# Block attention and a gated feed-forward in one kernel: score order in the opening, and weight casts on GpSimd

## The chip, the cores and the metric

The kernel runs on one core of one Trainium2 chip. The metric is the device time of one execution in microseconds (us). The engines are TensorE (PE; PEld is its weight load), VectorE (DVE), ScalarE (ACT), GpSimd (POOL) and SyncE (SP), which issues the DMAs. Each engine works off its own queue in order; engines wait for each other through semaphores.

## The reference

```python
# attention: q, k, v are [8, 8, 576, 64], float32; block = 64
scores = scale * np.matmul(q, k.transpose(0, 1, 3, 2))
scores = np.where(block_i >= block_j, scores, -1000000000.0)
attn = np.exp(scores - np.max(scores, axis=-1, keepdims=True))
attn = attn / (np.sum(attn, axis=-1, keepdims=True) + 1e-09)
x = np.matmul(attn, v)                      # heads side by side: [8, 576, 512]
# feed-forward
h = gelu_tanh(x @ w_in)                     # [8, 576, 1024]
u, v = h[..., :512], h[..., 512:]
v_n = (v - mean(v)) / np.sqrt(var(v) + 1e-06) * g_ln
v_s = np.einsum('ts,bsd->btd', w_sg, v_n) + b_sg[None, :, None]
out = x + (u * v_s) @ w_out
```

`w_in` and `w_out` arrive as float64, everything else as float32.

## The kernel before, in words

**Numbers.** TensorE multiplies in a rounded 32-bit format, so each operand is split into a high part (a cast) and a low part (the rest, a subtraction), and three products are summed. Such splits are `qh`, `ql`, `kh`, `kl` (`split_qk`, line 111), `xh`, `xl` (`Values.split`, line 469) and the weights' `wi_h`, `wi_l`, `ws_h`, `ws_l`, `wo_h`, `wo_l` (`split_weight`, line 183). A piece of 128x256 doubles is first turned into singles by `from_f64` (line 187): one ScalarE step (the absolute value, scaled) and three VectorE integer steps, the last of which needs ScalarE's. Then the cast on ScalarE and the subtraction on GpSimd.

**Slots.** The work goes through 32 slots, one for a pair of heads of one batch; four slots are a batch. Slot n holds:

- the transposes `pA`, `pB`, `pC` of slot n's probabilities, with their copies to SBUF (`Values.turn`);
- the inverse sums `r` on VectorE and their spread `rx` on GpSimd (`inverse`, line 408), transposed into `pd` and `pe` (`turn_sums`);
- the scores of slot n+1 in two halves, called here the first scores (row blocks 4, 1 and 0) and the second scores (blocks 3 and 2). Each half is followed by masked maxima on VectorE (`maximum`) and exponentials with sums on ScalarE (`exponent`). Both are in `Scores`, as `first` and `second`;
- the values' products `ob` and `pe`, and the normalised result `x` on VectorE (`products`, `normalise`);
- the split of q and k for slot n+2 on GpSimd (`split_qk`), and in the next slot the split of `x`.

From slot 4 on, the feed-forward of the batch before is laid between these on TensorE by `hole`: five groups `accv`, eight `accu`, eight `accs`, eight `acco`. Between `accv` and `accs` stands a layer norm: moments and `centre` on VectorE, the inverse deviation `rs` on GpSimd, `scale` to `vh` and `vl` on ScalarE and VectorE. The first four slots have no feed-forward to lay in; there the kernel puts eight idle transposes of the identity ahead of `pd` (`warm` in `turn_sums`).

**What sets the order.** Up to slot 3 the queues of TensorE, VectorE, ScalarE and GpSimd follow the program text (`written`, line 50). From slot 4 on only TensorE does; the others, and the DMA queue always, are ordered by the framework's scheduler. `issue_after` puts weight steps behind named instructions.

**Weights.** `load_share` (line 681) takes steps of a list of weight pieces at places of a slot that the table `WS` sets: two of the eight `v` pieces of `w_in` in each of slots 0 to 3, then the eight `u` pieces, the spatial weights, and `w_out`. `need` takes a step more when a feed-forward part starts: the first `u` piece comes that way, at the start of slot 4.

**Banks.** PSUM has eight banks in one ring (`bank`): a new tile waits until the readers of the tile eight places earlier are done. `pB` of a slot takes the bank of the slot before's `pe`, which `x` reads last.

Of the kernel before, what the change touches and what calls it, by code (L numbers as in the profile page):

```python
# [20 lines left out]
def kernel(  # L21
# [14 lines left out]
    P = 128  # L36
# [74 lines left out]
    def split_qk(n):  # L111
        out = []
        for x, t in zip(raw.pop(n), "qk"):
            hi = sp.tile([P, S], F32R, tag=t + "h", name=t + "h", bufs=1)
            lo = sp.tile([P, S], F32R, tag=t + "l", name=t + "l", bufs=1)
            if n == 0:
                copy("v" if t == "q" else "a", hi, x)
                vector.tensor_tensor(lo, x, hi.bitcast(F32), op=ALU.subtract)
            else:
                copy("g", hi, x)  # L120
                gpsimd.tensor_tensor(lo, x, hi.bitcast(F32), op=ALU.subtract)
# [65 lines left out]
    def from_f64(raw, dh, dl, name):  # L187

        n = raw.shape[-1]
        words = raw.bitcast(U32).rearrange("p (n t) -> p n t", t=2)  # L190
        hi, lo = words[:, :, 1], words[:, :, 0]
        tm = page(U32, 2 * n, name)
        t, m = tm[:, :n], tm[:, n:]


        scalar.activation(m.bitcast(F32), hi.bitcast(F32), AF.Abs, scale=2.0**-112)

        vector.tensor_scalar(t, lo, 29, None, op0=ALU.logical_shift_right)
        vector.scalar_tensor_tensor(
            t, hi, 0x80000000, t, op0=ALU.bitwise_and, op1=ALU.bitwise_or  # L200
        )
        vector.scalar_tensor_tensor(
            t, m, 3, t, op0=ALU.logical_shift_left, op1=ALU.bitwise_or
        )
        split_weight(t.bitcast(F32), dh, dl)

    def load_weight(src, cols, dh, dl, name="w", ahead=2):

        W = 256
        parts = [(c, slice(f, f + W)) for f in range(cols.start, cols.stop, W) for c in range(NC)]  # L210
        raws = {}

        def fetch(k):
            if k < len(parts):
                c, fs = parts[k]
                raws[k] = page(src.dtype, W, name)
                nc.sync.dma_start(raws[k], src[c * P : (c + 1) * P, fs])

        for k in range(ahead):
            fetch(k)  # L220
        for k, (c, fs) in enumerate(parts):
            fetch(k + ahead)
            args = (raws.pop(k), dh[:, c, fs], dl[:, c, fs])
            if src.dtype == F32:
                split_weight(*args)
            else:
                from_f64(*args, name)
            yield True

    def load_spatial():  # L230
# [20 lines left out]
        for j in range(NT - 1):  # L251
# [15 lines left out]

    weights = deque(
        [
            ("v", load_weight(w_in, slice(DH, DFF), wi_h, wi_l)),  # L270
            ("u", load_weight(w_in, slice(0, DH), wi_h, wi_l)),
            ("s", load_spatial()),
            ("o", load_weight(w_out, slice(0, DM), wo_h, wo_l, "xr", 0)),
        ]
    )

    def weight_step():

        while weights and next(weights[0][1], None) is None:
            weights.popleft()  # L280

    def need(part):

# [3 lines left out]

    spill = {}
    xs = {}
    behind = {}  # L290

    class Scores:

# [71 lines left out]
        def first(self, between=None):
            parts = ((4, 0, SH), (1, 0, EXT[1])), ((4, SH, S), (0, 0, EXT[0]))
            if between is None:
                for p in parts:
                    self.step(*p)
            else:  # L370
                for p in parts:
                    self.products(*p)
                between()
                for p in parts:
                    self.softmax(*p)
# [12 lines left out]
    class Values:  # L388
# [27 lines left out]
                r.unsqueeze(2).broadcast_to([P, NT * 2, D]),  # L416
            )

        def turn_sums(self, idle):

            def spread(i):
                return self.rx[:, i, :]

            t, t2 = bank("pd"), bank("pe")
            warm(t2, idle)
            for a in (0, 1):
                turn(t[:, a * BLK : a * BLK + P], prob[a][0])
            for i in (0, 1, 2):
# [249 lines left out]
    WS = [(0, 2, 0, 0), (0, 2, 0, 0), (0, 2, 0, 0), (0, 2, 0, 0), (0, 4, 0, 2), (0, 2, 0, 1)]
    WS += [(0, 2, 1, 0), (0, 0, 0, 3), (0, 2, 0, 3), (0, 0, 0, 0)]

    def load_share(n, k):

        if n < len(WS):
            with ExitStack() as order:
                if n >= H // 2:
                    for ins in behind.values():
                        order.enter_context(tc.issue_after(ins.ins))
# [6 lines left out]
    def slot(n, sc):  # L694
        va = Values(n, sc)
        nx = n + 1 < N
        q = H // 2
        k = 6 if n // q == 1 else 3
        if n == q:
            written.intersection_update("P")  # L700
        g = [int(x) for x in (FIRST if n // q == 1 else PLAN)[n % q]]
# [22 lines left out]
        if n < q:
            nx = Scores(n + 1)
            nx.first(lambda: va.turn_sums(8))
        else:
            va.turn_sums(0)
            hole(g[2])
            run_gelu()  # L730
        load_share(n, 1)
        if nx and n >= q:
# [85 lines left out]
```

## Time and profile before

| | |
|---|---|
| median of 3 runs | 782.54 us (781.96 to 782.93) |
| profiled execution | 783.17 us, of which the span from first to last instruction is 781.4 us |
| mean granted TensorE clock | 0.989 of full |
| busy share of the span | PE 97%, PEld 92%, DVE 62%, ACT 55%, POOL 40% |
| HBM | 83 GB/s over the span |

The busy shares are averages over stages with different limits. A row of the timeline reads: start, time busy, engine, line, operation, out<-in, shapes, count, and in brackets how long the engine stood idle before it and what released it. All engine instructions go through one helper and so show line 60; they are told apart by their tiles.

### The profile page before, as it was taken

Reading aid. Unit: us, or ns where it says so; the run is one execution under the profiler, and the core shown is the slowest. Engines: PE = TensorE matmul, PEld = TensorE weight load, DVE = VectorE, ACT = ScalarE, POOL = GpSimd, SP = SyncE. Lnnn points to the kernel's source line nnn. Section 1 sums busy time; section 2 is a strip of 40 time slices with the busy share of each in tenths; the row PEclk is TensorE's granted clock in tenths of the full one; section 3 lists DMA queues with packets and bytes.
Section 4 is the critical chain, followed back from the end, with each engine's and each line's share of the span. In section 5 each row is a group of like instructions: output and inputs, shape, how many; then the busy total and the mean of one; then the engine's idle time right before and its main releaser. Section 6 shows DMA issues by size and latency. Waiting matters only on the chain.

```text
span 781.4 us, 18302 instructions
## 1 busy us (share of the span) xinstructions
PE 758.7 (97%) x7138; PEld 716.0 (92%) x7138; DVE 483.4 (62%) x1477; ACT 428.0 (55%) x1093; POOL 313.8 (40%) x385
## 2 busy tenths in 40 slices
PE   8878898999999999999999999999999999999998
PEld 8777797999999899998999999998999989998998
DVE  6667678866966439563694447763496634942632
ACT  5666595848753477336682377533774358720600
POOL 3453666754435224453233534332344513322121
PEclk9989999999999999999999999999999999999999
DMA  6325232323241113421232222321225112120042
GB/s 219 118 91 168 64 98 70 91 72 117 81 151 62 59 42 98 138 62 36 73 108 93 61 62 62 130 85 33 61 79 166 49 45 61 61 78 16 1 122 91
DMA packets 46922, 65.84 MB, mean 84 GB/s; under 512 B 4082, under 2 KB 22514, under 8 KB 46836
## 3 DMA queue, kind: packets, MB, share of 16 engines
q1 hardware_dynamic: 46836, 64.67, 26.5%
q8 instruction: 56, 0.92, 0.5%
q14 instruction: 30, 0.25, 0.1%
HBM read 45.78 MB, written 18.87 MB: 83 GB/s over the span
## 4 chain that ended last, share of the span: by engine, by line
PE 86%; DVE 5%; ACT 4%; POOL 2%; DMA 2%; issue 1%; SPq 0%; ACTq 0%; POOLq 0%; DVEq 0%
PE accs L60 15%; PE acco L60 13%; PE accv L60 12%; PE accu L60 12%; PE s L60 10%; PE ob L60 9%; PE pB L60 4%; PE pC L60 4%; PE pA L60 3%; ACT prob L60 3%; PE pd L60 2%; DVE prob L60 2%; PE pe L60 2%; DMA w<-in_w_in 1%; DVE vv L550 1%
## 5 line engine op out<-in xcount | busy, mean ns | idle before, releaser
L60 ACT ACTIVATE prob<-prob,negm 128x576 f32<-128x576 f32 (+3 forms) x320 | 176.3, 553 | 57.9 <-DVE negm L60 55.1
L60 DVE CUSTOM_DVE_ANT_0 prob<-s,mask 128x288 f32<-128x288 f32 (+3 forms) x320 | 121.5, 424 | 51.7 <-PE s L60 51.2
L60 POOL TENSOR_TENSOR xh<-x,xh 128x64 fp32r<-128x64 f32 x32 | 13.9, 435 | 184.9 <-DVE xh L60 115.2
L60 POOL TENSOR_TENSOR gl<-u,gh 128x288 fp32r<-128x288 f32 x64 | 52.4, 823 | 87.0 <-DVE gh L60 86.7
L60 PE MATMUL accu<-xh,wi_h 128*128 128x288 f32 x256 | 78.8, 308 | 0.0
L60 PE MATMUL accs<-ws_h,vh 128*128 128x288 f32 x256 | 77.8, 304 | 0.0
L60 PE MATMUL acco<-gh,wo_h 128*128 128x288 f32 x256 | 77.6, 303 | 0.0
L60 PE MATMUL accu<-xl,wi_h 128*128 128x288 f32 x256 | 76.0, 297 | 0.0
L60 PE MATMUL accu<-xh,wi_l 128*128 128x288 f32 x256 | 75.7, 296 | 0.0
L60 PE MATMUL accs<-ws_h,vl 128*128 128x288 f32 x256 | 75.5, 295 | 0.0
L60 PE MATMUL acco<-gl,wo_h 128*128 128x288 f32 x256 | 75.5, 295 | 0.0
L60 PE MATMUL accs<-ws_l,vh 128*128 128x288 f32 x256 | 75.5, 295 | 0.0
L60 PE MATMUL acco<-gh,wo_l 128*128 128x288 f32 x256 | 75.3, 294 | 0.0
L60 PE MATMUL accv<-wi_h,xh 128*128 128x512 f32 x160 | 66.0, 412 | 1.7 <-DVE x L60 1.5
L60 DVE TENSOR_TENSOR u<-accs,u 128x288 f32<-128x288 f32 x64 | 29.2, 457 | 56.3 <-PE accs L60 55.0
L60 PE MATMUL accv<-wi_l,xh 128*128 128x512 f32 x160 | 63.6, 398 | 0.0
L60 PE MATMUL s<-kh,qh 64*128 64x288 f32 (+4 forms) x384 | 63.0, 322 | 0.2 <-DVE negm L60 0.2
L60 ACT ACTIVATION_READ_ACCUMULATOR prob<-prob,negm 128x1 f32 x320 | 60.0, 188 | 0.0
L60 PE MATMUL s<-kh,ql 64*128 64x288 f32 (+4 forms) x384 | 58.7, 301 | 0.0
L60 PE MATMUL s<-kl,qh 64*128 64x288 f32 (+4 forms) x384 | 57.7, 300 | 0.1
L60 POOL CAST kh<-k_f 128x576 fp32r<-128x576 f32 x31 | 22.0, 710 | 84.4 <-PE s L60 73.1
L60 ACT COPY vv<-accv 128x512 f32<-128x512 f32 x32 | 18.6, 580 | 64.9 <-PE accv L60 64.9
(115 smaller groups left out, 2139.2 us busy)
## 6 DMA issues: line engine op xcount, KB each, us to landing
q_f<-in_qT SPq DMA_DIRECT2D x32, 288.0 KB, 2.9
k_f<-in_kT SPq DMA_DIRECT2D x32, 288.0 KB, 2.8
spill<-x SPq DMA_DIRECT2D x32, 288.0 KB, 3.2
xr<-spill SPq DMA_DIRECT2D x32, 288.0 KB, 2.9
out_T<-xr SPq DMA_DIRECT2D x32, 288.0 KB, 2.1
v_f<-in_v SPq DMA_DIRECT2D x32, 256.0 KB, 3.5
w<-in_w_in SPq DMA_DIRECT2D x16, 256.0 KB, 4.3
xr<-in_w_out SPq DMA_DIRECT2D x8, 256.0 KB, 2.6
```

What stands on the lines that cost most here:

```text
L60: return lambda *a, **k: pin(method(*a, **k), self.letter)
L550: tc.keep_in_program_order(nc.vector.scalar_tensor_tensor(x, x, stats[:rows, st, 0:1], g_bc[:rows, :], op0=ALU.subtract, op1=ALU.mult))
```

## The change

Four things change.

1. In slots 0 to 2 the second scores and their softmax stand ahead of the values' products and of `x`. In slot 3 `x` and its split still come ahead of the second scores. The eight idle transposes go. `opening_slot` is a function of its own now.
2. A weight piece is opened (loads, and the ScalarE step of a double) in one step and finished (three VectorE steps, cast, subtraction) in a second one. In slots 0 to 3 the opening stands behind `turn_sums` and ahead of the exponentials, and the finishing behind the first maxima. The eight `v` pieces are taken 3, 2, 2 and 1 a slot, not 2 a slot, and one more is loaded ahead.
3. The cast of a weight's high part goes from ScalarE to GpSimd, for all weights.
4. The inverse sums of slot n+1 are written ahead of the split of q and k at the end of slot n, from the end of slot 3 on; weight steps from slot 4 on are put behind the last GpSimd step of such a split, too. The table `WS` moves two pieces from slot 6 to slot 5.

```diff
     def split_weight(x, dh, dl):
-        scalar.copy(dh, x)
+        gpsimd.tensor_copy(dh, x)
         gpsimd.tensor_tensor(dl, x, dh.bitcast(F32), op=ALU.subtract)
...
+            opened = []
+            for j in range(k, k + size):
+                fetch(j + ahead)
+                raw = raws.pop(j)
+                opened.append(raw if src.dtype == F32 else Double(raw, name))
+            yield False
+            for j, x in zip(range(k, k + size), opened):
+                c, fs = parts[j]
+                split_weight(
+                    x if src.dtype == F32 else x.single(), dh[:, c, fs], dl[:, c, fs]
+                )
+            k += size
             yield True
...
-            ("v", load_weight(w_in, slice(DH, DFF), wi_h, wi_l)),
+            ("v", load_weight(w_in, slice(DH, DFF), wi_h, wi_l, "w", 3, (3, 2, 2, 1))),
...
-    WS = [(0, 2, 0, 0), (0, 2, 0, 0), (0, 2, 0, 0), (0, 2, 0, 0), (0, 4, 0, 2), (0, 2, 0, 1)]
-    WS += [(0, 2, 1, 0), (0, 0, 0, 3), (0, 2, 0, 3), (0, 0, 0, 0)]
+    WS = {
+        4: (0, 4, 0, 2),
+        5: (0, 5, 0, 0),
+        6: (0, 1, 0, 0),
+        7: (0, 0, 0, 3),
+        8: (0, 2, 0, 3),
+    }
...
+    def opening_slot(n, va):
+
+        va.turn(0, "A")
+        va.turn(1, "A")
+        split_pending()
+        va.turn(0, "B")
+        va.turn(1, "B")
+        va.inverse()
+        va.turn(0, "C")
+        va.turn(1, "C")
+        load_v(n + 1)
+        load_qk(n + 2)
+        nx = Scores(n + 1)
+        for p in nx.FIRST:
+            nx.products(*p)
+        va.turn_sums()
+        weight_half()
+        for p in nx.FIRST:
+            nx.softmax(*p)
+        weight_half()
+        if n < Q - 1:
+            nx.second()
+            va.products()
+            va.normalise()
+            pending.append(va.split)
+        else:
+            va.products()
+            va.normalise()
+            va.split()
+            nx.second()
+        nv = Values(n + 1, nx)
+        if n == Q - 1:
+            nv.inverse()
+        split_qk(n + 2)
+        return nx, nv
...
-        if n >= q:
-            va.inverse()
...
+        nv = None
+        if nx:
+            nv = Values(n + 1, nx)
+            nv.inverse()
         if n + 2 < N:
             split_qk(n + 2)
```

`Double` holds what `from_f64` did, in two parts: making one issues ScalarE's step, its `single` the three steps on VectorE. `weight_half` takes one of the two steps of a group of pieces.

On VectorE, the end of slot 1's weight steps and what follows. Before (`w` are the integer steps of a weight piece, `x` the result, the `ISA` rows the second maxima):

```order
L60 SCALAR_TENSOR_TENSOR w<-w 128x256 x2
L60 TENSOR_TENSOR x<-ob,rb 128x512
L60 TENSOR_TENSOR x<-pe,rb 128x64
L60 ISA prob_3_111,negm<-s,mask 128x448
L60 ISA negm 128x1
L60 ISA prob_3_121,negm<-s,mask 128x448
```

Now, in the same place:

```order
L60 SCALAR_TENSOR_TENSOR w<-w 128x256 x2
L60 ISA prob_3_111,negm<-s,mask 128x448
L60 ISA negm 128x1
L60 ISA prob_3_121,negm<-s,mask 128x448
L60 ISA negm 128x1
L60 ISA prob_2_109,negm<-s,mask 128x320
L60 ISA negm 128x1
L60 ISA prob_2_119,negm<-s,mask 128x320
L60 ISA negm 128x1
L60 TENSOR_TENSOR x<-ob,rb 128x512
```

The maxima of the second scores moved ahead of `x`, and no longer wait for the products that `x` reads.

On GpSimd, the same slot: `rx` are slot 1's inverse sums, `wi_l` the low parts of weights, `qh` to `kl` the split that slot 2's first scores read. Before:

```order
L60 COPY rx<-r 128x640
L60 MEMSET sums 128x2
L60 TENSOR_TENSOR wi_l<-w,wi_h 128x256 x2
L60 CAST qh<-q_f 128x576
L60 TENSOR_TENSOR ql<-q_f,qh 128x576
L60 CAST kh<-k_f 128x576
L60 TENSOR_TENSOR kl<-k_f,kh 128x576
```

Now:

```order
L60 COPY rx<-r 128x640
L60 MEMSET sums 128x2
L60 CAST wi_h<-w 128x256
L60 TENSOR_TENSOR wi_l<-w,wi_h 128x256
L60 CAST wi_h<-w 128x256
L60 TENSOR_TENSOR wi_l<-w,wi_h 128x256
L60 CAST qh<-q_f 128x576
L60 TENSOR_TENSOR ql<-q_f,qh 128x576
```

Two casts came in ahead of the split; the rest of the queue kept its order.

On GpSimd in slot 4: `xh`, `xl` split the last `x` of batch 0, `rx` are slot 4's inverse sums, `qh` to `kl` the split for slot 5, the `wi_l` rows weight pieces. Before:

```order
L60 TENSOR_TENSOR xl<-x,xh 128x576
L60 CAST qh<-q_f 128x576
L60 MEMSET sums 128x2
L60 TENSOR_TENSOR wi_l<-w,wi_h 128x256
L60 TENSOR_TENSOR ql<-q_f,qh 128x576
L60 CAST kh<-k_f 128x576
L60 COPY rx<-r 128x640
L60 TENSOR_TENSOR wi_l<-w,wi_h 128x256 x4
L60 TENSOR_TENSOR kl<-k_f,kh 128x576
```

Now:

```order
L60 TENSOR_TENSOR xl<-x,xh 128x576
L60 MEMSET sums 128x2
L60 COPY rx<-r 128x640
L60 CAST qh<-q_f 128x576
L60 TENSOR_TENSOR ql<-q_f,qh 128x576
L60 CAST kh<-k_f 128x576
L60 TENSOR_TENSOR kl<-k_f,kh 128x576
L60 CAST wi_h<-w 128x256 x4
L60 TENSOR_TENSOR wi_l<-w,wi_h 128x256 x4
```

`rx` and the whole split moved ahead of the weight pieces; the casts of those pieces are new on this queue.

On VectorE at the end of slot 6's transposes, where the layer norm of batch 0 is scaled (`vone`, `vn_t`, `vl`) and `xr` is the first piece of `w_out`. Before:

```order
L60 COPY ptC<-pC 128x512
L60 TENSOR_SCALAR vone<-vv,rs 64x512
L60 TENSOR_TENSOR ws_l<-xr,ws_l 1x576
L60 CAST vn_t<-vone 64x512
L60 SCALAR_TENSOR_TENSOR vn_t<-vv,rs,vone 64x512
```

Now:

```order
L60 COPY ptC<-pC 128x512
L60 TENSOR_TENSOR ws_l<-xr,ws_l 1x576
L60 TENSOR_SCALAR xr<-xr 128x256
L60 SCALAR_TENSOR_TENSOR xr<-xr 128x256 x2
L60 TENSOR_SCALAR vone<-vv,rs 64x512
L60 CAST vn_t<-vone 64x512
```

The three steps of a `w_out` piece moved ahead of the layer norm's scaling.

More of the change, by code (lines that the diff above doesn't have):

```diff
@@ L101 @@
     v_bufs = []
+    behind = {}
     def load_qk(n):
@@ L120, in split_qk @@
                 copy("g", hi, x)
[L121 removed]
+                behind["G"] = gpsimd.tensor_tensor(lo, x, hi.bitcast(F32), op=ALU.subtract)
             out += [hi, lo]
@@ L183, in split_weight, with __init__, single, load_weight @@
     def split_weight(x, dh, dl):
-        scalar.copy(dh, x)
+        gpsimd.tensor_copy(dh, x)
         gpsimd.tensor_tensor(dl, x, dh.bitcast(F32), op=ALU.subtract)
[L187 to L207, printed above, removed]
+    class Double:
+        def __init__(self, raw, name):
+            n = raw.shape[-1]
+            words = raw.bitcast(U32).rearrange("p (n t) -> p n t", t=2)
+            self.hi, self.lo = words[:, :, 1], words[:, :, 0]
+            tm = page(U32, 2 * n, name)
+            self.t, self.m = tm[:, :n], tm[:, n:]
+            scalar.activation(
+                self.m.bitcast(F32), self.hi.bitcast(F32), AF.Abs, scale=2.0**-112
+            )
+        def single(self):
+            t = self.t
+            vector.tensor_scalar(t, self.lo, 29, None, op0=ALU.logical_shift_right)
+            vector.scalar_tensor_tensor(
+                t, self.hi, 0x80000000, t, op0=ALU.bitwise_and, op1=ALU.bitwise_or
+            )
+            vector.scalar_tensor_tensor(
+                t, self.m, 3, t, op0=ALU.logical_shift_left, op1=ALU.bitwise_or
+            )
+            return t.bitcast(F32)
+    def load_weight(src, cols, dh, dl, name="w", ahead=2, groups=()):
         W = 256
@@ L220, in load_weight @@
             fetch(k)
[L221 to L227, printed above, removed]
+        k = 0
+        for size in (*groups, *([1] * len(parts))):
+            if k == len(parts):
+                return
+            opened = []
[8 more added lines that the diff above has]
+                    x if src.dtype == F32 else x.single(), dh[:, c, fs], dl[:, c, fs]
+                )
+            k += size
             yield True
@@ L275, with weight_half @@
     )
+    def weight_half():
+        while weights:
+            said = next(weights[0][1], None)
+            if said is not None:
+                return said
+            weights.popleft()
     def weight_step():
-        while weights and next(weights[0][1], None) is None:
-            weights.popleft()
+        while weight_half() is False:
+            pass
     def need(part):
@@ L363, in softmax, with first @@
                         self.exponent(a, i)
[L365 to L375, printed above, removed]
+        FIRST = ((4, 0, SH), (1, 0, EXT[1])), ((4, SH, S), (0, 0, EXT[0]))
+        def first(self):
+            for p in self.FIRST:
+                self.step(*p)
         def second(self):
@@ L417, in inverse, with turn_sums @@
             )
-        def turn_sums(self, idle):
+        def turn_sums(self):
             def spread(i):
@@ L676, in hole @@
                 work.popleft()
[L678 to L679 removed]
+    WS = {
[5 more added lines that the diff above has]
+    }
     def load_share(n, k):
[L683 removed]
+        if n in WS:
             with ExitStack() as order:
[L685 to L687 removed]
+                for ins in behind.values():
+                    order.enter_context(tc.issue_after(ins.ins))
                 for _ in range(WS[n][k]):
@@ L692, with split_pending, slot @@
     FIRST = ["1112", "1111", "1111", "2114"]
-    def slot(n, sc):
-        va = Values(n, sc)
-        nx = n + 1 < N
[L697 to L701, printed above, removed]
+    Q = H // 2
+    def split_pending():
+        for f in pending:
+            f()
+        pending.clear()
+    def opening_slot(n, va):
[32 more added lines that the diff above has]
+        return nx, nv
+    def slot(n, va):
+        nx = n + 1 < N
+        k = 6 if n // Q == 1 else 3
+        g = [int(x) for x in (FIRST if n // Q == 1 else PLAN)[n % Q]]
         if n + 1 < N:
@@ L711, in slot @@
         run_side(k)
-        for f in pending:
-            f()
-        pending.clear()
+        split_pending()
         load_share(n, 0)
@@ L723, in slot @@
         va.turn(1, "C")
[L724 to L730, printed above, removed]
+        va.turn_sums()
+        hole(g[2])
+        run_gelu()
         load_share(n, 1)
-        if nx and n >= q:
+        if nx:
             nx = Scores(n + 1)
@@ L764 @@
     warm(bank("warm"), 16)
+    va = Values(0, sc)
     for n in range(N):
-        sc = slot(n, sc)
+        if n == Q:
+            written.intersection_update("P")
+        sc, va = (opening_slot if n < Q else slot)(n, va)
         if n % (H // 2) == H // 2 - 1:
```

13 lines of the change are left out of this document (5 added, 8 removed).

## The prediction

> **What bounds the kernel now.** I read the busy time and granted clock of each slot first, then TensorE's waits up to 140 us, then the chain of work that ended last inside one opening slot, then the timeline of single engines. In the table of windows (start:end, length, busy us of PE, PEld, DVE, ACT, POOL, then clock, DMA share and GB/s), slot 0's end, slot 1, slot 4, slot 6 and everything from 161 us on:
>
> ```profile
> 11.50:21.50 10.00, 9.78 (x131) 9.06 (x130) 5.42 (x23) 7.53 (x26) 2.53 (x4) 1.00 0.42 137
> 21.50:36.80 15.30, 12.60 (x142) 11.50 (x139) 10.51 (x38) 9.34 (x30) 8.07 (x10) 0.89 0.41 125
> ...
> 67.50:97.80 30.30, 25.37 (x191) 20.65 (x188) 23.07 (x69) 17.93 (x54) 15.90 (x20) 0.94 0.41 128
> ...
> 114.50:136.30 21.80, 18.16 (x181) 17.06 (x180) 18.03 (x45) 12.75 (x31) 14.30 (x12) 0.92 0.27 80
> ...
> 161.20:781.40 620.20, 616.64 (x5726) 586.55 (x5725) 365.57 (x1100) 322.22 (x799) 223.53 (x261) 1.00 0.25 77
> ```
>
> From 161 us on TensorE is busy 616.64 of 620.20 us at full clock, and none of its work there goes: that part stays. What can change is ahead of it, where TensorE waits and its clock falls:
>
> ```profile
> PE pd L60 <- POOL rx L60: 5.4, 2, 3.4
> PE pB L60 <- DVE x L60: 4.6, 3, 1.6
> PE pB L60 <- ACT prob L60: 3.6, 4, 1.1
> ```
>
> Why slots 1 to 3 last about 15.3 us is in the chain of slot 1 (start, us, what):
>
> ```profile
> 31.00 1.02 PE pe L60 x8
> 32.03 0.56 PE pd L60 x5
> ...
> 33.47 3.06 ACT prob L60 x12
> 36.53 0.33 ACT w L60
> ...
> 36.88 0.44 DVE w L60
> ...
> 37.75 0.34 ACT w L60
> ...
> 38.11 0.72 DVE w L60
> 38.83 0.73 DVE x L60 x2
> ...
> 40.14 0.77 ACT prob L60 x2
> ...
> 40.95 1.31 PE pB L60 x9
> 42.26 1.95 PE pC L60 x10
> ```
>
> ScalarE does the six first exponentials (3.06 us), then passes a weight piece to VectorE and back, twice (36.53 to 38.83); `x` and the second maxima stand behind that; only then come the second exponentials, at 40.14. Those 3.6 us from 36.53 are a detour for weights that nobody needs before slot 4.
>
> **The opening (slots 0 to 3).** With the second maxima ahead of `x` and the weights' ScalarE step ahead of the exponentials, the detour leaves this chain. What is late next? The rows of slot 1 (and `s`, the first scores, of slot 0, and `kl` ahead of slot 3):
>
> ```profile
> 14.06 0.40 PE L60 MATMUL s<-kh,qh 64*128 64x288 f32 x2
> ...
> 24.77 0.66 POOL L60 CAST qh<-q_f 128x576 fp32r<-128x576 f32 x1
> ...
> 27.84 1.41 POOL L60 TENSOR_TENSOR kl<-k_f,kh 128x576 fp32r<-128x576 f32 x1
> ...
> 30.36 0.46 DVE L60 CUSTOM_DVE_ANT_0 prob<-s,mask 128x288 f32<-128x288 f32 x1 [0.30 <-PE s L60]
> ...
> 30.84 0.72 POOL L60 COPY rx<-r 128x640 f32<-128x640 f32 x1
> ...
> 32.91 0.29 DVE L60 TENSOR_SCALAR w<-w 128x256 uint32<-128x256 uint32 x1
> ...
> 58.60 1.41 POOL L60 TENSOR_TENSOR kl<-k_f,kh 128x576 fp32r<-128x576 f32 x1
> ```
>
> and what single steps take (VectorE's as shortest/median/longest ns; GpSimd's as count, busy us, mean ns):
>
> ```profile
> L60 DVE SCALAR_TENSOR_TENSOR w<-w x32: 407/424/1636, 17.9 to 100.1; 128x256 uint32<-128x256 uint32 x32
> L60 DVE TENSOR_SCALAR w<-w x16: 277/291/1190, 17.6 to 96.9; 128x256 uint32<-128x256 uint32 x16
> ```
>
> ```profile
> L60 POOL TENSOR_TENSOR wi_l<-w,wi_h 128x256 fp32r<-128x256 f32 x16 | 11.8, 751 | 30.8 <-ACT wi_h L60 30.8
> L60 POOL TENSOR_TENSOR xl<-x,xh 128x576 fp32r<-128x576 f32 x6 | 8.5, 1421 | 0.0
> L60 POOL CAST qh<-q_f 128x576 fp32r<-128x576 f32 x8 | 5.5, 682 | 5.7 <-DMA q_f<-in_qT 5.7
> ```
>
> I count from K, the end of `kl`, which the first scores need: 29.25 in slot 1. VectorE's first maxima end and its weight steps begin at 32.91, K+3.66. A piece costs VectorE 0.29+0.42+0.42 = 1.13. Then GpSimd: the cast is not in the trace on this engine; 682 ns for 576 columns bounds it from above, 256/576 of it, 0.30, from below, and I take 0.35, near the scaled row since the other GpSimd rows scale with columns too (0.751 against 1.421). With the subtraction's 0.75 a piece costs GpSimd 1.10. (At 0.68 the seven casts of slots 0 to 2 would cost 2.3 us more, within the wider bound below.) Behind the pieces stands the split, 4.48 from the start of `qh` (24.77) to the end of `kl`. So the next K, two pieces a slot:
>
> - if VectorE's second piece runs beside GpSimd's first: 3.66+1.13+2x1.10+4.48 = 11.5;
> - if the engines shut each other out and take turns: 3.66+2x(1.13+1.10)+4.48 = 12.6.
>
> The rows speak for something between: VectorE's step took up to 1636 ns against 424, so it does get shut out at times. The Trainium skill, "SBUF — State Buffer", section "Who interferes with whom", says that a VectorE instruction with two SBUF inputs contends with a GpSimd instruction that reads SBUF, and the later one fully blocks. It speaks against moving the cast here: by it the turn-taking sum holds throughout, and the whole would come out at about 771.2. I take 12.0 for two pieces. Slot 0 with three: 12.6 or 14.8, I take 13.5.
>
> The other chain is shorter. GpSimd's `rx` ends at K+2.31; `pd` to the first exponential is 1.44 (32.03 to 33.47); two weight steps on ScalarE 0.68; exponentials 3.06; the second ones start by K+7.5, and from there `pC` ended 4.07 later (40.14 to 44.21) with the clock partly down: K+11.6, or about 10.6 with `pC` at a full clock. `pB` waits for the bank that `x` frees, at 3.66+2.26+2.0 (four maxima of some 0.5, by the 0.46 above)+0.73 = K+8.7, within the same time. The eight idle transposes (1.02) lay beside `rx`; their going frees nothing.
>
> Slot 0's first scores start at 14.06, as K = 13.96. So K of slot 3 falls at 13.96+13.5+2x12.0 = 51.5, where it was 58.60+1.41 = 60.0: **8.5 us gained** (6.0 with turns taken, 10.4 side by side).
>
> In slot 3 one `v` piece is left, but the first `u` piece now stands ahead of `x` on VectorE, and its load is issued behind that of `k_f`, which waits for `kl`: at about K+0.8, an estimate. From issue to landing loads take (us, last column):
>
> ```profile
> w<-in_w_in SPq DMA_DIRECT2D x16, 256.0 KB, 4.3
> xr<-in_w_out SPq DMA_DIRECT2D x8, 256.0 KB, 2.6
> ```
>
> It is there at K+5.1, but its last VectorE step needs ScalarE, which is free of exponentials at K+7.2 and done at 7.6. So: `x` 8.0 to 8.8, `xh` and `xl` on GpSimd until K+11.0 (1.42 for `xl`), and slot 4's first `accv` group, held by `xl`, ends at K+11.7. Before, it ended at 74.98, K+15.0: **3.3 us more**. The casts freed from ScalarE are worth nothing by themselves: it idles.
>
> **Slot 4.**
>
> ```profile
> 74.98 1.25 PE L60 MATMUL pB<-ident,prob 128*128 128x128 f32 x10
> ...
> 82.35 0.55 PE L60 MATMUL pd<-ident,rx 128*128 128x128 f32 x3 [2.04 <-POOL rx L60]
> ...
> 97.82 0.60 PE L60 MATMUL pA<-ident,prob 128*128 128x128 f32 x4
> ```
>
> From 74.98 to 97.82 TensorE waits 2.04 us for `rx`, and a clock of 0.94 over 30.3 us costs 1.8. Now `rx` comes ahead of split and weights: up to 3.8 gained. But the split is now behind `rx`, which waits for the inverse, which on VectorE is behind a piece whose load is behind the spill of `x`: ready near K+15, split done near K+20.5, just when the first scores want it. I take **3.0** (1.5 to 3.8).
>
> **Slot 6.** The same wait was 3.4 us there, with a clock of 0.92 over 21.8 us (1.7). Yet the chain that ended last runs not through it but through the layer norm:
>
> ```profile
> 119.47 4.43 DVE vv L550 x5
> ...
> 124.56 0.24 POOL rs L60
> ...
> 126.92 1.17 POOL rs L60
> ...
> 128.62 0.76 DVE ws_l L60
> ```
>
> So taking the wait away gives nothing while that chain stays. It gets the three steps of a `w_out` piece ahead of `vone`: their load (2.6) starts when the `ws_l` subtraction that stands ahead of the second `rs` row frees its page, so they end about 1.2 to 2.5 us after `rs`, and only `ws_l`'s 0.76 goes out of the way. **I take -1.0** (+1.5 to -2.5).
>
> The other casts on GpSimd (the `u` pieces, the spatial weights, `w_out`) cost nothing as long as its idle time covers them: 7.5 of 21.8 us in slot 6. Without that cover each costs 0.35 to 0.68. The inverse ahead of the split in later slots, the two moved pieces and the deeper prefetch: nothing, under TensorE's full load.
>
> **Sum.** 8.5+3.3+3.0-1.0 = 13.8 us. The profiled execution took 783.17, a span of 781.4 and 1.8 around it; it would take 769.4. The median, 782.54, is 0.63 lower: **768.7 us**. My bounds: 15.7 to 11.3 from the opening's two ends, up to 3.3 more and 3.0 less from the slots behind: 763.5 to 774.2.
>
> **Rivals.**
>
> *ScalarE's chain sets the opening, not GpSimd's* (chance 0.10). For: 11.6 and 11.5 are close, and the clock may stay up. Then a slot takes 10.6, K of slot 3 is 45.8, 5.7 us earlier: 763.0. Against: every step of the split and the pieces is in one queue.
>
> *The feed-forward takes it back* (0.12). `rx` in slot 4 waits for the loads as long as it did, and the `w_out` piece holds ScalarE's and VectorE's layer norm 4 us: 11.8-4 = 7.8 gained, 774.7. For: both pieces now wait for loads in queues that others need. Against: the loads have the 4.3 and 2.6 us used above.
>
> *The clock falls in the opening: slower* (0.03). Without idle transposes TensorE may be granted half the clock. A slot's work is 9.8 us (9.78 in the first window, without `pA`, with the 1.02 idle ones, about as much): 19.6 at half clock. Then slot 3's K is 72.8, 12.8 later than before, and 790.0 comes out. It decides from 56% of the work at half clock on, where 9.8x1.56 = 15.3. For: a clock of 0.89 already. Against: the waits that brought it go. The Trainium skill, "TensorE: Matmul & The Clock Gate", section "What's actually happening", has the clock halved after an idle window of about 3.4 us; this trace contradicts it, with 0.89 at gaps of 1.6 at most. By that rule the chance would be nil.
>
> *The order is changed, but the bound stays* (0.03): the first maxima hold the banks of the second scores, slots stay at 15.3, and only slots 4 and 6 count: 2.0 gained, 780.5.
>
> **Chances and range.** The forecast has 0.72. Inside 763.5 to 774.5 lies all of it and some of its neighbours. A measurement here can tell 0.2%, 1.6 us. Faster: 0.72+0.10+0.12 and most of the last rival, 0.96; slower 0.03; same 0.01.
>
> **What would show it.** Right: opening slots near 12 us; `pB` no longer waiting for `x` behind weight steps; GpSimd without a gap from the first weight cast to `kl`, and the first scores starting at its end; no wait of `pd` for `rx` in slots 4 and 6, but waits for maxima or layer norm in slot 6. Wrong: GpSimd idle ahead of `kl` in the opening, a clock under 0.85 there, or new TensorE waits behind 161 us.

## The result, and the profile after

| | before | after |
|---|---|---|
| median | 782.42 us (781.96 to 782.93, 4 runs) | 773.67 us (770.57 to 776.39, 4 runs) |
| profiled execution, its span | 783.17, 781.4 us | 773.07, 771.2 us |
| TensorE busy, mean granted clock | 97%, 0.989 | 98%, 0.989 |

The ratio is 0.9887, with a 95% interval of 0.9848 to 0.9925: 8.8 us gained, where 13.8 were forecast. The runs of the new kernel lie 5.8 us apart, those of the old one 1.0.

The table of windows of the kernel after (start:end, length, busy us of PE, PEld, DVE, ACT, POOL, clock, DMA share, GB/s). I cut it at slot 0's first scores, at the ends of `kl` after slots 0, 1 and 2 (the prediction's K), then at the first `pA` of a slot: slots 0, 1 and 2, slot 3's rest with slot 4, slots 5, 6 and 7, and all that follows.

```profile
14.75:28.52 13.77, 11.01 (x136) 9.47 (x135) 11.95 (x43) 9.59 (x30) 8.54 (x13) 1.00 0.41 122
28.52:40.88 12.36, 11.75 (x131) 10.32 (x131) 10.32 (x36) 8.13 (x27) 8.81 (x13) 0.86 0.34 99
40.88:52.82 11.94, 10.51 (x133) 9.17 (x131) 11.01 (x41) 8.66 (x28) 8.97 (x13) 1.00 0.46 146
52.82:84.22 31.40, 30.79 (x286) 26.74 (x287) 23.72 (x79) 18.10 (x56) 20.90 (x32) 0.95 0.44 135
84.22:100.58 16.36, 16.35 (x181) 15.60 (x180) 11.79 (x42) 15.28 (x39) 14.33 (x19) 1.00 0.37 103
100.58:126.48 25.90, 20.97 (x181) 19.52 (x180) 22.13 (x54) 12.77 (x34) 15.05 (x15) 0.80 0.25 76
126.48:151.14 24.66, 24.66 (x244) 24.15 (x243) 20.13 (x57) 15.58 (x41) 16.60 (x20) 1.00 0.22 67
151.14:771.20 620.06, 616.56 (x5726) 586.46 (x5724) 354.30 (x1100) 321.01 (x793) 220.74 (x268) 1.00 0.25 77
```

The same view of the kernel before, cut in the same way (slot 3's rest with slot 4, slot 6, and all from slot 8 on):

```profile
60.01:97.82 37.81, 32.88 (x300) 27.66 (x299) 27.15 (x90) 22.63 (x69) 18.33 (x27) 0.95 0.36 112
...
114.50:136.37 21.87, 18.23 (x181) 17.13 (x180) 18.10 (x46) 12.82 (x31) 14.37 (x12) 0.92 0.27 80
...
161.29:781.40 620.11, 616.55 (x5726) 586.46 (x5724) 365.48 (x1100) 322.22 (x799) 223.44 (x261) 1.00 0.25 77
```

From slot 8 on the two are the same (620.11 and 620.06 us), so the difference is made ahead of it and can be counted: K of slot 3 comes 7.2 earlier (60.01 to 52.82), from there to slot 5 6.4 are gained, in slots 5 and 7 0.3 each, and slot 6 gives 4.0 back. That is 10.2, the difference of the spans.

TensorE's waits of the kernel after, the main ones up to 140 us:

```profile
PE pd L60 <- POOL rx L60: 3.4, 1, 3.4
PE s L60 <- POOL kl L60: 1.9, 2, 1.0
...
PE accu L60 <- DVE negm L60: 1.3, 1, 1.3
PE pB L60 <- DVE negm L60: 0.9, 1, 0.9
```

`pB` waits no longer for `x`, and the first scores wait for `kl`. But one wait for `rx` is left, as long as before: slot 6's. GpSimd there, in the kernel after (in brackets the idle time ahead and its releaser):

```profile
104.77 0.67 POOL L60 CAST ws_h<-xr 128x576 fp32r<-128x576 f32 x1 [2.41 <-DMA xr<-in_w_sgT]
105.39 4.03 POOL L60 TENSOR_TENSOR kl<-k_f,kh 128x576 fp32r<-128x576 f32 x1
109.37 1.18 POOL L60 COPY rx<-r 128x640 f32<-128x640 f32 x1
110.51 1.40 POOL L60 TENSOR_TENSOR ql<-q_f,qh 128x576 fp32r<-128x576 f32 x1
112.00 0.63 POOL L60 TENSOR_SCALAR rs<-stats 128x5 f32<-128x5 f32 x1
112.70 1.41 POOL L60 TENSOR_TENSOR ws_l<-xr,ws_h 64x576 fp32r<-64x576 f32 x1
114.08 1.20 POOL L60 TENSOR_TENSOR rs<-rs,half 128x5 f32<-128x5 f32 x1
```

And VectorE:

```profile
103.20 0.20 DVE L60 RECIPROCAL r<-r 128x10 f32<-128x10 f32 x1
...
105.47 4.50 DVE L564 SCALAR_TENSOR_TENSOR vv<-vv,stats,g_bc 128x512 f32<-128x512 f32 x5
...
115.98 0.29 DVE L60 TENSOR_SCALAR xr<-xr 128x256 uint32<-128x256 uint32 x1 [3.45 <-POOL rs L60]
116.31 0.96 DVE L60 SCALAR_TENSOR_TENSOR xr<-xr 128x256 uint32<-128x256 uint32 x2
117.18 0.47 DVE L60 TENSOR_SCALAR vone<-vv,rs 64x512 fp32r<-64x512 f32 x1
```

`r` is there at 103.40, but `rx` starts at 109.37: ahead of it in GpSimd's queue stand the cast of the last spatial piece, which waits 2.41 for its load, and `kl`, which takes 4.03 beside the five centre steps of the layer norm. `rx` ends 9.97 us into the slot. In the kernel before, where `ql`, drawn out to 4.29, stood ahead of it:

```profile
119.06 4.29 POOL L60 TENSOR_TENSOR ql<-q_f,qh 128x576 fp32r<-128x576 f32 x1
123.30 1.18 POOL L60 COPY rx<-r 128x640 f32<-128x640 f32 x1
...
126.88 1.19 POOL L60 TENSOR_TENSOR rs<-rs,half 128x5 f32<-128x5 f32 x1
```

That `rx` ended 9.98 us into its slot (124.48 less 114.50). So nothing was won there, and what follows came later: `ql` now lies between `rx` and `rs`, so that `rs` ends 14.70 into the slot (115.28 less 100.58), where it was 13.57 (126.88 and 1.19, less 114.50). The `w_out` piece then holds `vone` another 1.9 (0.7 of it until its load is there, at 115.97), and the maxima behind `vone` come so late that `accu` waits 1.3 for their banks. TensorE is busy 2.7 us longer for the same 181 matmuls, at a clock of 0.80 for 0.92, and idle 1.3 longer: the 4.0.

### The profile page after: what moved, and what is told of

Its sections match the earlier page's. It is cut to its first block, busy times and chain, and to the rows that moved or that the text cites. A ratio compares the mean times of both kernels' runs of the same rounds, so it can differ in the third digit from the quotient of the medians.

```text
span 771.2 us, 18236 instructions
## 1 busy us (share of the span) xinstructions
PE 755.3 (98%) x7106; PEld 713.0 (92%) x7106; DVE 473.4 (61%) x1477; ACT 417.4 (54%) x1064; POOL 320.7 (42%) x414
## 4 chain that ended last, share of the span: by engine, by line
PE 91%; POOL 3%; DVE 3%; ACT 1%; issue 1%; DMA 1%; SPq 0%; POOLq 0%; DVEq 0%; ACTq 0%
PE accs L60 16%; PE accv L60 14%; PE acco L60 13%; PE accu L60 13%; PE ob L60 10%; PE s L60 10%; PE pB L60 4%; PE pC L60 4%; PE pA L60 3%; PE pd L60 2%; PE pe L60 1%; DVE prob L60 1%; ACT prob L60 1%; POOL kl L60 1%; DMA xr<-in_w_sgT 1%
## 5 line engine op out<-in xcount | busy, mean ns | idle before, releaser
L60 POOL TENSOR_TENSOR xh<-x,xh 128x64 fp32r<-128x64 f32 x32 | 10.5, 327 | 185.6 <-DVE xh L60 113.5
L60 PEld LDWEIGHTS accu<-xh,wi_h 128*128 128x128 f32 x256 | 49.2, 192 | 2.9 <-issue 1.5
```

Of the source, the lines that this page charges most:

```text
L60: return lambda *a, **k: pin(method(*a, **k), self.letter)
```

## The experiments

My theory: the opening goes by GpSimd's loop from `kl` to `kl`; slot 6 gives time back because weight pieces stand in GpSimd's and VectorE's queues ahead of `rx` and of the layer norm. Rivals: the casts as such cost slot 6 its time; ScalarE's chain or the clock sets the opening. In the table each kernel's median, its ratio to the kernel before with the 95% interval, and from its profile the lengths of slots 0, 1 and 2 (slot 0 from its first scores to K, then K to K), of slot 3's rest with slot 4, and of slots 5, 6 and 7. The kernels ran in several rounds, each with runs of the kernel before (medians of 782.0 to 783.5); a ratio is taken within its round.

| kernel | median | ratio | slots 0, 1, 2 | 3 and 4 | 5 | 6 | 7 |
|---|---|---|---|---|---|---|---|
| before | 782.42 | 1 | 15.19, 15.24, 15.52 | 37.81 | 16.68 | 21.87 | 24.92 |
| after | 773.67 | 0.9887 (0.9848 to 0.9925) | 13.77, 12.36, 11.94 | 31.40 | 16.36 | 25.90 | 24.66 |
| after, again | 774.80 | 0.9907 (0.9888 to 0.9927) | 13.78, 12.45, 11.94 | 30.98 | 16.35 | 25.84 | 24.71 |
| old table | 770.76 | 0.9848 (0.9830 to 0.9866) | 13.77, 12.21, 12.14 | 30.98 | 16.34 | 22.84 | 25.45 |
| late casts on ScalarE | 771.79 | 0.9865 (0.9845 to 0.9885) | 13.77, 12.32, 11.91 | 31.44 | 16.68 | 23.83 | 25.53 |
| opening's casts on ScalarE | 771.67 | 0.9865 (0.9847 to 0.9882) | 14.11, 14.35, 13.72 | 30.77 | 16.13 | 20.99 | 24.99 |
| before, inverse ahead | 785.62 | 1.0037 (1.0023 to 1.0051) | 15.19, 15.49, 14.95 | 41.11 | 16.67 | 21.86 | 24.94 |
| before, inverse ahead, weights behind | 779.57 | 0.9952 (0.9939 to 0.9965) | 15.18, 15.22, 15.53 | 34.36 | 16.68 | 21.88 | 24.71 |
| old table, `rs` whole | 770.28 | 0.9839 (0.9827 to 0.9852) | 13.78, 12.35, 13.92 | 31.00 | 16.34 | 22.18 | 25.40 |
| no extra piece | 770.86 | 0.9852 (0.9833 to 0.9871) | 13.77, 12.34, 13.91 | 31.51 | 16.13 | 23.50 | 24.60 |
| idle transposes back | 769.89 | 0.9843 (0.9828 to 0.9859) | 13.86, 12.32, 12.01 | 31.10 | 16.12 | 16.52 | 33.35 |
| late casts on ScalarE, idle transposes | 771.53 | 0.9847 (0.9833 to 0.9861) | 13.89, 12.29, 12.04 | 31.04 | 16.68 | 24.41 | 25.05 |
| combined | 764.24 | 0.9756 (0.9743 to 0.9769) | 13.87, 12.31, 12.01 | 30.03 | 17.32 | 17.45 | 24.60 |
| combined, two pieces each | 761.85 | 0.9726 (0.9714 to 0.9739) | 12.26, 12.04, 12.03 | 30.02 | 17.35 | 17.44 | 24.61 |

### The changed kernel again

> The changed kernel once more. Its four runs lay between 770.57 and 776.39 us, those of the kernel before between 781.96 and 782.93. Theory (the stall of slot 6 is what varies, since there GpSimd's whole queue hangs on the landing of one load): slot 6, 25.90 us in the first profile, is longer or shorter here by about as much as the profiled time differs from 773.07, and the opening slots stay within 0.3 us. Rival (the spread comes from the opening, where VectorE and GpSimd take turns as chance has it): slot 6 stays at 25.9 and the opening slots of 13.82, 12.36 and 11.97 differ.

The median was 774.80 (772.48 to 776.94, 6 runs). Slot 6 repeated itself to 0.06 us and the opening slots to 0.1, so neither the theory nor the rival is borne out; but the two profiled executions, 773.07 and 772.48, lie only 0.6 apart, too close to show what makes the 6 us. Two later profiles show a part of it, since all up to slot 2 is the same code in them. This is slots 1 and 2 of the kernel with the old table and `rs` whole:

```profile
27.99:40.34 12.35, 11.73 (x119) 10.61 (x120) 8.93 (x34) 8.00 (x26) 8.72 (x13) 0.72 0.32 94
40.34:54.26 13.92, 11.98 (x145) 10.23 (x143) 13.04 (x43) 9.11 (x29) 9.05 (x13) 1.00 0.39 130
```

With a clock of 0.72 in slot 1 its `pA` comes later, VectorE's copies reach into slot 2, and slot 2 lasts 13.9, not 11.9. The ten runs of the changed kernel had mean clocks of 0.986 to 0.991, and the three longest of them (776.39, 776.77, 776.94) 0.986. Where their clock fell stays open: only profiled runs show it. The six at 0.991 still lie between 770.57 and 775.26, so the mean clock isn't all of it.

### The old table in slots 5 and 6

```diff
-        5: (0, 5, 0, 0),
-        6: (0, 1, 0, 0),
+        5: (0, 2, 0, 1),
+        6: (0, 2, 1, 0),
```

> The table gives slot 5 three pieces and slot 6 three again, as before; all else as changed. Theory (in slot 6 the cast of the last spatial piece waits for its load ahead of kl and rx, and the w_out piece stands ahead of the layer norm; 25.90 us where the kernel before had 21.87): both go behind rx and the layer norm, slot 6 falls to 21 to 22.5, TensorE's wait of 3.4 for rx goes, and the median falls by 3 to 5 to 768.5 to 771. Rival (the casts fill GpSimd wherever they stand, 15.05 of 25.90 us busy): slot 6 stays within 1 us of 25.9, 773 to 775. Second rival (two more pieces in slot 6 cost VectorE 1.1 us each on its path): 775 to 776.

The median was 770.76, as the theory has it, and slot 6 fell by 3.0 to 22.84, 0.3 above the theory's range. The subtractions of the spatial pieces moved behind `rx`, the `w_out` piece out of the slot, and TensorE no longer waits for `rx` there (but 3.3 for the maxima, which now come behind `vone`). The new longest idle time on VectorE is the layer norm's:

```profile
111.72 0.87 DVE L60 TENSOR_SCALAR vone<-vv,rs 64x512 fp32r<-64x512 f32 x1 [3.25 <-POOL rs L60]
```

### Late casts on ScalarE

```diff
-    def split_weight(x, dh, dl):
-        gpsimd.tensor_copy(dh, x)
+    def split_weight(x, dh, dl, e="a"):
+        copy(e, dh, x)
...
+                    "g" if groups else "a",
...
-        gpsimd.tensor_copy(ws_h[:, j, :], t)
+        scalar.copy(ws_h[:, j, :], t)
```

> Casts of all weights but the eight v pieces go back to ScalarE; the opening keeps them on GpSimd. Theory (order, not the casts' work): the subtraction of the last spatial piece still stands ahead of kl and rx on GpSimd and still waits for the same load, so slot 6 stays at 24.5 to 26 and the median at 772 to 774. Rival (the casts as such cost it): slot 6 falls to the 21.87 of before, 769 to 770.

Slot 6 came to 23.83 and the median to 771.79, between the two. TensorE still waits 1.7 for `rx`, but for another reason: the inverse sums themselves are late. On VectorE the last spatial piece and a `w_out` piece stand ahead of them, and the first step of the latter waits for its load:

```profile
105.07 0.37 DVE L60 TENSOR_SCALAR xr<-xr 128x256 uint32<-128x256 uint32 x1 [1.16 <-DMA xr<-in_w_out]
...
107.70 0.19 DVE L60 RECIPROCAL r<-r 128x10 f32<-128x10 f32 x1
```

`r` ends 7.0 into the slot here (107.89 less 100.90), where it ended 2.8 into it in the changed kernel. The edit changed the work and, by way of the scheduler, the order, so it can't tell the two apart.

### The opening's casts on ScalarE

```diff
-    def split_weight(x, dh, dl):
-        gpsimd.tensor_copy(dh, x)
+    def split_weight(x, dh, dl, e="g"):
+        copy(e, dh, x)
...
+                    "a" if groups else "g",
```

> Only the eight v pieces are cast on ScalarE again; the later weights keep GpSimd. Theory (GpSimd's loop from kl to kl sets an opening slot): the casts stand behind six exponentials on ScalarE, some 7.5 us after kl, so GpSimd begins its subtractions that late: two of them (1.5) and the split (4.5) end 13.8 after kl, slots of 13.5 to 14.5 in place of 12 to 12.4, the opening 5 to 7 us longer, median 778 to 781. Rival (ScalarE's chain sets it): ScalarE gets 0.35 a piece more, 2 to 3 us in all, 776 to 777. If neither is on the path: 773 to 774.

The opening did what the theory says: slots 1 and 2 took 14.35 and 13.72 (13.5 to 14.5 expected), 2.0 and 1.8 more than with the casts on GpSimd; GpSimd stands idle there until ScalarE's cast is done. Slot 0 was only 0.3 longer, so the opening grew by 4.1, not by 5 to 7. In slot 1:

```profile
36.84 1.42 POOL L60 TENSOR_TENSOR wi_l<-w,wi_h 128x256 fp32r<-128x256 f32 x2 [6.17 <-ACT wi_h L60]
38.21 0.89 POOL L60 CAST qh<-q_f 128x576 fp32r<-128x576 f32 x1
```

But the median fell to 771.67, where 778 or more was expected: slot 6 took 20.99 in place of 25.90. Its instructions are those of the changed kernel, but the scheduler put the steps of the `w_out` piece between and behind the maxima, and the load of the spatial piece was there when GpSimd came to it. I hadn't expected that an edit of the opening moves 4.9 us in slot 6; why the scheduler ordered it otherwise isn't shown.

### The inverse alone, and with the weights behind

```diff
+        if nx:
+            nv = Values(n + 1, nx)
+            if n >= q - 1:
+                nv.inverse()
         if n + 2 < N:
             split_qk(n + 2)
```

> The kernel before with one part of the change: from the end of slot 3 on the inverse sums are written ahead of the split of q and k. Theory (rx first in GpSimd's queue is all that shortens slot 4): the opening stays as before, slot 4 falls from 22.84 to 19 to 19.5, slot 6 stays within 1 us of its 21.87 since its layer norm sets it, median 778 to 779. Rival (slot 4 got shorter because the shorter opening let loads and casts come in time): slot 4 stays at 22 or more, 781 to 782.

It got slower, 785.62, which neither the theory nor the rival has. Slot 4's wait for `rx` went, but TensorE's first scores wait for the split instead:

```profile
86.02 0.40 PE L60 MATMUL s<-kh,qh 64*128 64x288 f32 x2 [2.36 <-POOL kh L60]
87.50 0.61 PE L60 MATMUL s<-kl,qh 64*128 64x288 f32 x2 [0.95 <-POOL kl L60]
```

On GpSimd four weight pieces had come between `qh` and `ql`, ahead of `kh`:

```profile
79.94 0.86 POOL L60 CAST qh<-q_f 128x576 fp32r<-128x576 f32 x1
80.77 3.23 POOL L60 TENSOR_TENSOR wi_l<-w,wi_h 128x256 fp32r<-128x256 f32 x4
83.96 1.39 POOL L60 TENSOR_TENSOR ql<-q_f,qh 128x576 fp32r<-128x576 f32 x1
```

The second kernel adds the other half, in `split_qk`:

```diff
-                gpsimd.tensor_tensor(lo, x, hi.bitcast(F32), op=ALU.subtract)
+                behind["G"] = gpsimd.tensor_tensor(lo, x, hi.bitcast(F32), op=ALU.subtract)
```

> The kernel before with both halves of the last item of the change: the inverse sums ahead of the split, and the weight steps from slot 4 on behind the last GpSimd step of such a split. The half alone made slot 4 longer, 33.2 us from its first transposes to the next, against 30.2, since rx and one cast went ahead and five weight pieces kept kh and kl back (2.4 us of waiting of the first scores for kh). Theory (it takes both): kh and kl come ahead of the pieces, slot 4 falls to 27 to 28.5, slot 6 stays near 21.9, median 779 to 780.5. Rival (slot 4 gets shorter only after a shorter opening): 30 or more, 782 or more.

With the weight steps behind the split, 779.57, and slot 4 (first `pA` to the next) at 26.78, down from 30.21: the theory. The inverse needs the weights behind the split, and no shorter opening; the weights' half alone wasn't run. In slot 6 this kernel waits for `rx` as before, its `rx` ends 9.98 into the slot again, and the slot takes 21.88: the earlier inverse moves nothing there.

### `rs` whole

```diff
-            gpsimd.tensor_scalar(rs, stats[:, :, 1], 1e-6, None, op0=ALU.add)
+            vector.tensor_scalar(rs, stats[:, :, 1], 1e-6, None, op0=ALU.add)
```

> The changed kernel with the old table's slots 5 and 6, and the layer norm's adding of 1e-6 on VectorE, so that GpSimd has one step for rs and no spatial piece can come between its two. Theory (with the old table the layer norm's chain sets slot 6: VectorE idles 3.25 us for rs, behind two ws_l of 1.4 to 1.6 us each): that idle time goes, slot 6 falls from 22.84 to 19.5 to 20.5, below the 21.87 of the kernel before, and the median from 770.8 to 767 to 769. Rival (something else in slot 6 is as late: the maxima, the transposes' copies, the ws_l behind it that the first accs needs): slot 6, or slot 7 behind it, stays long, 770 to 771.

The rival: 770.28, slot 6 at 22.18. VectorE no longer waits for `rs`; but GpSimd's two spatial steps now run beside the layer norm's centre steps, and both take longer. VectorE:

```profile
106.84 5.73 DVE L564 SCALAR_TENSOR_TENSOR vv<-vv,stats,g_bc 128x512 f32<-128x512 f32 x5
```

GpSimd:

```profile
108.60 3.42 POOL L60 TENSOR_TENSOR ws_l<-xr,ws_h 128x576 fp32r<-128x576 f32 x2
```

With the old table alone the five steps took 3.37, so the 3.25 us of idle time turned into 2.4 us of contention.

### No extra piece

```diff
-        while any(p == part for p, _ in weights):
-            weight_step()
+        if weights and weights[0][0] == part:
+            for _ in weights.popleft()[1]:
+                pass
```

> The start of a feed-forward part finishes its own weight pieces but takes none of the next list: the u piece leaves the end of slot 3, the w_out piece leaves slot 6, and each later piece comes one place later. Theory: in slot 3 x no longer waits 2.20 us for ScalarE's step, but TensorE's products end only 0.8 us before x starts, so slot 4's first group comes 0.5 to 0.9 earlier; in slot 6 vone follows rs at once, not 1.9 us later, while the wait for rx behind the late load stays: slot 6 at 23.5 to 24.5, median 771 to 772.5. Rival (the w_out piece is all that is wrong in slot 6): slot 6 falls to 21 to 22, 769 to 770. Rival on the other side (the later pieces now crowd slots 7 to 9): 774 or more.

The median was 770.86 and slot 6 23.50, about the theory's numbers, but not by its path. `vone` is no longer held by the `w_out` piece, and the wait of `pd` for `rx` fell to 1.0; in its place stands a wait of 3.9 of `ob` for `ptC`, whose copy is late on VectorE behind a step of the last spatial piece that waits 4.22 for ScalarE. Slots 3 and 4 together gained nothing, where 0.5 to 0.9 was expected.

### The idle transposes

```diff
             t, t2 = bank("pd"), bank("pe")
+            if self.n < Q:
+                warm(t2, 8)
```

> The changed kernel with the eight idle transposes ahead of pd in slots 0 to 3 put back. Theory (they lie beside rx, and GpSimd's loop sets a slot): opening slots as they are, 13.8, 12.4 and 12.0, the granted clock in slot 2 up from 0.86 but nothing gained, median 773 to 775. Rival (without them the clock falls, and that keeps an opening slot from 11.5): slots shorter by 0.3 to 0.8, 771 to 773. Other side (they push pd and all behind it back by 1.0 a slot): 776 to 778.

The median was 769.89, below what any of the three expected: but in this kernel the scheduler had also moved the maxima of slot 6 ahead of `vone` (slot 6 16.52, slot 7 33.35), so it tells nothing by itself. The next one does, with the same order as the kernel with the late casts on ScalarE:

> The kernel with the late casts on ScalarE (771.79 us) plus the eight idle transposes in slots 0 to 3; on VectorE, ScalarE and GpSimd the same instructions in the same order. Theory (the idle transposes hold TensorE's clock, whose falls to 0.72 to 0.86 in some opening slots make the next slot up to 2 us longer): clock 1.00 in all opening slots, 1 to 2 us less, median 769.5 to 771, runs closer together. Rival (what 769.89 us owed to the idle transposes was the other order in slots 6 and 7 that came with them): no gain, 771.3 to 772.3.

771.53 against 771.79: no gain that can be told (by the ratios, each within its round, up to 1.4 us, but their intervals overlap), though the clock is now 1.00 in each opening slot:

```profile
14.27:28.16 13.89, 11.88 (x144) 10.34 (x143) 12.00 (x43) 9.57 (x30) 8.56 (x13) 1.00 0.48 152
28.16:40.45 12.29, 11.32 (x139) 10.06 (x139) 10.29 (x38) 8.34 (x27) 8.94 (x13) 1.00 0.39 121
40.45:52.49 12.04, 11.12 (x139) 10.06 (x139) 10.30 (x38) 8.35 (x27) 8.98 (x14) 1.00 0.32 98
```

Slots 1 and 2 are as long as without the idle transposes (12.29 and 12.04, against 12.32 at a clock of 0.86 and 11.91 at 1.00); only behind the clock of 0.72 seen above did a slot grow. In this pair the idle transposes bring the runs closer together (1.0 us, against 3.3); with the idle transposes alone they still lay 2.9 apart. Why the kernel with the idle transposes alone reached 769.89 isn't shown: its profiled run, at 772.34, was the longest of its four.

### All together

```diff
+    def split_weight(x, dh, dl, e="a"):
+        copy(e, dh, x)
...
+                    "g" if groups else "a",
...
+            t, t2 = bank("pd"), bank("pe"); self.n < Q and warm(t2, 8)
+        if weights and weights[0][0] == part:
+            for _ in weights.popleft()[1]:
+                pass
```

> Late casts on ScalarE, the idle transposes, and no extra piece at the start of a feed-forward part. On GpSimd in slot 6 the two steps of rs stand side by side and rx ahead of them; the w_out piece is gone from there. Theory (slot 6 is lost to queue order): slot 6 falls from 23.83 to 20 to 21.5, the opening gains 1 to 2 by the clock, median 765.5 to 768. Rival (VectorE's own work sets slot 6, its centre and vl steps beside GpSimd): slot 6 at 22 or more, 768.5 to 770.5.

764.24, better than expected: slot 6 takes 17.45 at full clock. GpSimd there:

```profile
102.22 1.42 POOL L60 TENSOR_TENSOR ws_l<-xr,ws_h 64x576 fp32r<-64x576 f32 x1 [0.20 <-ACT ws_h L60]
103.60 2.01 POOL L60 TENSOR_TENSOR ql<-q_f,qh 128x576 fp32r<-128x576 f32 x1
105.56 0.71 POOL L60 COPY rx<-r 128x640 f32<-128x640 f32 x1
106.66 0.65 POOL L60 TENSOR_SCALAR rs<-stats 128x5 f32<-128x5 f32 x1 [0.39 <-DVE stats L60]
107.39 1.55 POOL L60 TENSOR_TENSOR rs<-rs,half 128x5 f32<-128x5 f32 x1
```

The last spatial piece is through before the layer norm's steps begin, so those aren't stretched (3.36), and `rx` ends 5.9 into the slot. Which of the three edits brought this order isn't shown: with one or two of them slot 6 took 23.5 to 24.4, or 16.5 with slot 7 at 33.4.

```diff
-            ("v", load_weight(w_in, slice(DH, DFF), wi_h, wi_l, "w", 3, (3, 2, 2, 1))),
+            ("v", load_weight(w_in, slice(DH, DFF), wi_h, wi_l, "w", 2, (2, 2, 2, 2))),
```

> The same with the eight v pieces two in each of slots 0 to 3, not 3, 2, 2 and 1; from slot 4 on the same. Theory (GpSimd's loop sets slot 0 too, and slot 3 has room): slot 0 shorter by 1.5 to 2.2, slot 3 up to its x longer by 0 to 1.1, 0.5 to 2 less than the kernel with 3, 2, 2 and 1. Rival (slot 0 is set by TensorE and the softmax): no difference, or up to 1.1 more.

761.85: 2.4 less. The third piece of slot 0 had cost 1.6 (13.87 for 12.26), and the second one of slot 3 costs nothing (30.02 for 30.03); the first scores also started earlier in this profile, at 13.87 for 14.87, which they do by chance elsewhere too (13.9 to 14.9 in the profiles of all kernels). This version beats both kernels, by some 21 and 12 us. Its slot 0:

```profile
13.87:26.13 12.26, 11.36 (x144) 10.34 (x143) 10.68 (x40) 9.14 (x29) 7.36 (x11) 1.00 0.47 142
```

## Why the prediction was right, and where it was not

The time of the profiled execution was to be 769.4 and was 773.1. The 3.7 between them: 1.3 in the opening, 3.0 in slot 6, less some 0.7 gained elsewhere. The median came out 0.6 above the profiled execution, where 0.6 below had been assumed; that is the rest between 768.7 and 773.67.

**The opening (8.5 forecast, 7.2 measured).** The mechanism held in the main: the loop from `kl` to `kl` through VectorE's weight steps and GpSimd's queue. Two pieces were to take 12.0 us, between 11.5 and 12.6, and took 12.36 and 11.94; three pieces were to take 13.5 from the first scores and took 13.8; the cast took 0.40, estimated at 0.35. So 0.6 of the miss is size, and 0.7 a later start: the first scores came at 14.75, not 14.06, which varies from profile to profile.

ScalarE was counted as off this path, and isn't quite. In slot 1 VectorE's weight steps began at K+3.28, not K+3.66, but their third step waited for ScalarE's, which stands behind `pd` and `pe`, on a half clock there; GpSimd's cast follows:

```profile
33.26 0.42 DVE L60 SCALAR_TENSOR_TENSOR w<-w 128x256 uint32<-128x256 uint32 x1 [0.71 <-ACT w L60]
...
33.75 0.40 POOL L60 CAST wi_h<-w 128x256 fp32r<-128x256 f32 x1 [2.88 <-DVE w L60]
```

With the clock at 1.00 (late casts on ScalarE, idle transposes) that wait was 0.47 in slot 1 and 0.18 in slot 2. And "the casts freed from ScalarE are worth nothing by themselves" doesn't hold: from slot 0's first scores to K of slot 3 it is 45.95 before, 42.18 with the opening's casts on ScalarE and 38.07 after, so the casts' move to GpSimd makes 4.1 of it, and the rest of the change in the opening (the order, the two-step weights and their share of 3, 2, 2, 1, no idle transposes) together 3.8. The parts of that rest weren't run apart.

The forecast's ends were 1.10 for a further piece side by side, and 2.23 in turns; the third piece of slot 0 cost 1.6 (13.87 for 12.26). By the Trainium skill, "SBUF — State Buffer", section "Who interferes with whom", the later one of two such instructions on VectorE and GpSimd fully blocks. Taken as turns throughout, as in the prediction, that is 2.23, so the trace agrees only in part.

**Slots 3 and 4 (6.3 forecast, 6.4 measured).** 3.3 and 3.0 were forecast, and 2.6 and 3.8 came: `accv`'s first group ends at 65.21, K+12.4 for K+11.7, and slot 4 from there to its end takes 19.01, where it took 22.84. `x` came at K+8.2, as counted, but `xl` was through at K+11.7, not K+11.0; and the clock was at 0.80 ahead of slot 4 (in the repeat, at 1.00 there, the group ended at K+12.0). That the inverse pays only with the weights behind the split isn't in the prediction; it counted them as one edit; the runs show 3.3 us lost by the one (41.11 for 37.81) and 3.4 gained by both (34.36).

**Slot 6 (-1.0 forecast, -4.0 measured).** This step failed. "No wait of `pd` for `rx` in slots 4 and 6" was right for slot 4 alone: I read GpSimd's queue in slot 4 and took it to be the same in slot 6, where a cast that waits for its load and the split still stand ahead of `rx`. Of the layer norm's chain I counted what a `w_out` piece costs (1.2 to 2.5; it was 1.9) and credited 0.8 for VectorE's `ws_l`, but not `ql` between `rx` and `rs` (1.1), nor the low clock that follows both waits. With the old table slot 6 is 1.0 longer than before, the forecast's number: but that kernel's table is not the change's.

**The rivals.** ScalarE's chain: as a bound it fell (its slot of 10.6 didn't come), though it adds up to 0.7 to the loop, as above. The feed-forward takes it back, with 4 us in the layer norm: the 4 us came in slot 6, but only 1.9 of them from the `w_out` piece, while its other half, `rx` of slot 4 waiting for the loads, did not; that its 774.7 is near the median is chance. The clock in the opening: it fell, to 0.86 and at times 0.72, without gaps over 1.0 us, but cost some 2 us in two profiles, not 13. The order without effect: fell.

## What to carry to other kernels

Read the queue of an in-order engine at each place on which a term rests: the same edit made room in one slot and none in another, and an instruction that waits for a load holds everything behind it. Where a scheduler orders the queues, a small edit far away can be worth more than the one under study (4.9 us here), so compare orders before comparing times. An edit with two halves may cost by one and gain by both; time them apart.

## What the runs showed of the hardware

VectorE and GpSimd, both reading two tiles of SBUF, took together nearly the sum of their times: `kl` (1.41 alone) and five centre steps (3.36 alone) were through in 4.6 us side by side, and both were drawn out to 4.03 and 4.50; neither was simply first.

The granted clock fell to one half behind short waits (0.95 us at most), in steps of 3.4 us. Slot 1 of the kernel after, the stretch ahead of the fall and the fall itself:

```profile
27.59:31.00 3.41, 1.91 (x25) 1.60 (x24) 2.08 (x10) 0.00 (x0) 3.28 (x5) 1.00 0.86 254
31.00:34.41 3.41, 3.41 (x19) 2.62 (x21) 2.62 (x13) 2.33 (x9) 0.58 (x2) 0.50 0.21 62
```

In the kernel with the opening's casts on ScalarE a like fall began at 28.68. The third stretch of 3.41 us behind that, and the one that follows it:

```profile
38.92:42.33 3.41, 1.79 (x16) 1.32 (x14) 2.25 (x4) 1.98 (x6) 3.25 (x4) 1.00 0.38 115
42.33:45.74 3.41, 2.45 (x27) 2.00 (x28) 2.26 (x13) 0.07 (x1) 2.70 (x5) 1.00 0.42 131
```

With TensorE busy 1.91 of 3.41 us the next 3.41 us ran at half clock, with 1.79 in the other kernel they didn't: the busy time alone doesn't say when the clock falls, and what does isn't shown. The Trainium skill, "TensorE: Matmul & The Clock Gate", section "What's actually happening", has a window of that length, and the half clock after an idle one: the length agrees, but this one wasn't idle.
